# Neighbouring matmuls into different PSUM banks, in a fused attention, expert and gated-MLP kernel

## The chip, the cores and the metric

The kernel runs on one core of a Trainium2 chip. The metric is the device time in microseconds (us) of that core for one execution of the whole program. Times in the trace are counted from the start of its span; durations of single instructions are in nanoseconds (ns). The engines are PE (TensorE matmul), PEld (TensorE weight load), DVE (VectorE), ACT (ScalarE), POOL (GpSimd) and SP (the queue that issues most transfers).

## What is computed

Three layers follow one another, all in float32.

```python
# attention by features: q, k, v are 4 x 8 x 576 x 64, w_phi is 64 x 128
q_p, k_p = phi(q), phi(k)                    # exp(+-proj) with the row's maximum taken off
num = q_p @ (k_p.T @ v); den = q_p @ sum(k_p)
x = num / (den + 1e-6)                       # as 2304 tokens x 512

# 8 experts, two to a token, 512 -> 1024 -> 512
for e in range(8):
    h = maximum(x[mask] @ w1[e], 0.0)
    out[mask] += top2_w[mask] * (h @ w2[e])

# gated MLP over all tokens, 512 -> 1536 -> 512
xn = x / sqrt(mean(x * x) + 1e-6) * rms_g
g = xn @ w_gate
y = (g * sigmoid(g) * (xn @ w_val)) @ w_out
```

## The kernel before

Every large product is made of three matmuls for each pair of blocks: both operands are split into a high and a low part (`split`, line 120: ACT makes the high part, DVE the low part by subtraction), and high x high, high x low and low x high are added up in PSUM. Since 128 x 128 blocks are the stationary operand, each matmul has its own weight load.

PSUM is used in whole banks. `bank` (line 110) hands out 512-column tiles under two tags, np with five buffers and acc with three, each in rotation: a new tile takes the buffer of the tile of that tag that lies five (or three) calls back, and waits until that tile's last reader is done.

The work is issued in an order written out by hand. A long list (lines 24 to 46) orders attention and routing; from line 1168 on, loops do. Each engine takes its instructions strictly in that order, and so does SP's queue of transfers.

The first expert layer has 8 experts with two units of tokens each, of three and two tiles of 128 tokens. `s1_chunk` (line 786) makes one of 8 chunks of hidden values in one np bank. `s2_chunk` (line 804) adds chunk f to the unit's output, which has one acc bank for each tile of tokens; it finishes the three matmuls of a tile before it turns to the next tile. `y_out` (line 816) copies the banks out, DVE and ACT by turns, and POOL scatters the rows to `y_d`.

The gated MLP works on nine groups of 256 tokens. For each group, twelve calls of `g_chunk` (line 961) make 128 gate features and 128 value features each: one np bank holds both halves, the twelve matmuls of the gate half (L970) come first, those of the value half after them. Then ACT takes the sigmoid of the gate half (L974), and DVE multiplies it by the gate half (L975) and by the value half (L976). `g_split` (line 979) splits the product of the chunk before. Then `o_chunk` (line 984) adds chunk by chunk to the output of 128 tokens, in an acc bank for each of the group's two tiles (j): three matmuls (L991) for j = 0, three for j = 1, and so on. In the last group the steps are sorted, so that all of j = 0 is done before j = 1. `store` (line 994) copies an output and sends it out.

The MLP's weights are loaded during the last experts and the first group: `w_load` (line 664) issues the transfer on SP's queue, `w_hi` (line 682) makes the high part on ACT (for gate and value in four pieces scaled by the norm's weights, L691), `w_lo` (line 696) the low part on DVE (L702). In the loop over the first group's chunks they stand in the order `g_chunk(f)`, `g_split(f - 1)`, `w_lo`, `w_hi`, `w_load` (lines 1233 to 1242). The rows of the second group are fetched by `gather2(1)` (line 1230), ahead of the first group's chunks, from the rows that the experts have scattered.

Of the kernel before, what the change touches and what calls it, by code (L numbers as in the profile page):

```python
# [15 lines left out]
AF = mybir.ActivationFunctionType  # L16
# [5 lines left out]

# the order of attention and routing: each name stands for its function's next call
ORDER = """
# [25 lines left out]
def moe_stack_kernel(  # L50
# [17 lines left out]
    nc = tc.nc  # L68
# [41 lines left out]
    def bank(tag, *shape):  # L110
        n = 1
        for d in shape:
            n *= d
        t = ps.tile([P, 512], F32, name=tag, bufs=BUFS[tag])[:, 0:n]
        return t.rearrange("p (a b) -> p a b", a=shape[0]) if len(shape) > 1 else t
# [7 lines left out]

    # features 128 i + 32 kk + r lie at partitions 32 i + r where vector transposes make the operand
    def w1_src(e, kk):
# [6 lines left out]

    # ---------------------------------------------------------------- attention and routing
    aq_s, ak_s = ExitStack(), ExitStack()
# [47 lines left out]

    # the tensor engine's clock rises with use: products of no account until the first loads land
    warm = aq.tile([P, 512], BF16, name="warm")
# [53 lines left out]

    # An item is eight (head, token tile) blocks. k: heads of a quad, two tiles, or all heads of
    # a tail tile; q likewise. T transposes, H and L their two parts, P projection, M maximum,  # L240
    # U their maximum over features, X features, Z and Y sums of features, C contraction,
    # G, B and V copies, Q a tail's share, F the state by features; for queries V copies,
    # A maximum and S its subtraction, C contraction, N division.
    tps, xts, pps, pms, kp, kpt, acc, kvz = {}, {}, {}, {}, {}, {}, {}, {}
# [123 lines left out]

    # a head's columns: state by dimension, by the router's weights, feature sums
    def kF(it, c):  # L370
# [15 lines left out]

    # features of two heads a tile: pair i's heads A and B, or all pairs' head i for a tail
    def qP(it, i):
# [36 lines left out]

    # numerators, logits and denominators by tokens: a tile of the item, or half the heads of a tail
    def qC(it, i):
# [161 lines left out]

    # a pair's token row; an empty slot reads row 0  # L590
    def row_ids(ids, r):
# [6 lines left out]

    # ---------------------------------------------------------------- slots beyond CAP
    def overflow():  # L600
# [36 lines left out]

    # ---------------------------------------------------------------- experts
    nu = 2 * KF2 // 2 + KF2 // 2
# [22 lines left out]

    # an expert's unit lands in a tile of its own, the gated MLP's in the second half of its slot
    def w_load():
# [68 lines left out]
    ixs, rxs = (ix0, ix1), (rx0, rx1)  # L733
    # quarter rows by partitions 32 i + t: quarter i of the tokens of slots t
    rq = sp_.tile([P, E - 1, CAP // 32], I32, name="rq")
    quart = sp_.tile([P, 1], I32, name="quart")
    x_q = x_d.rearrange("t (i f) -> (t i) f", i=4)
    # an expert's units: 3 and 2 tiles, for expert 0 the smaller first
    groups = [(e, u) for e in range(E) for u in range(2)]
# [27 lines left out]

    # blocks of 32 transposed: features by partitions
    def turn(t, i, x, y):
# [16 lines left out]
    def s1_chunk(n, f):  # L786
        e, u = groups[n]
        N = P * NTL[n]
        t = xT[n][0]
        hp = bank("np", N)  # L790
        # the tokens' low parts are there last
        for m, (c, kk, a) in enumerate([(0, kk, a) for kk in range(KD) for a in range(2)]
                                       + [(1, kk, 0) for kk in range(KD)]):
            nc.tensor.matmul(hp, lhsT=slot1(e, kk)[:, a, f * P:(f + 1) * P], rhs=t[:, kk, c, :],  # L794
                             start=(m == 0), stop=(m == 3 * KD - 1))
        h = mp.tile([P, 2, NU0], F32R, name="hT", bufs=KF)[:, :, 0:N]
        nc.scalar.activation(out=h[:, 0, :], in_=hp, func=AF.Relu)  # L797
        nc.vector.scalar_tensor_tensor(out=h[:, 1, :], in0=hp, scalar=0.0, in1=f32(h[:, 0, :]),  # L798
                                       op0=ALU.max, op1=ALU.subtract)
        hT[n, f] = h  # L800
# [3 lines left out]
    def s2_chunk(n, f):  # L804
        e, u = groups[n]
        if f == 0:
            yacc[n] = [bank("acc", 512) for _ in range(NTL[n])]
        w = slot1(e, 4 + f // 2)
        h = hT.pop((n, f))
        o = (f % 2) * DM  # L810
        for i in range(NTL[n]):
            for m, (a, c) in enumerate(((0, 0), (0, 1), (1, 0))):
                nc.tensor.matmul(yacc[n][i], lhsT=h[:, a, i * P:(i + 1) * P], rhs=w[:, c, o:o + DM],  # L813
                                 start=(f == 0 and m == 0), stop=(f == KF - 1 and m == 2))
# [14 lines left out]

    # float64 weights arrive as pairs of words: exponent and fraction move to float32's places,  # L830
    # and what lies below float32's normal range becomes zero
    c64 = {}
# [49 lines left out]

    # ---------------------------------------------------------------- gated MLP
    NG2 = TT // 2
# [48 lines left out]

    # by way of DRAM: partitions 32 q + t take quarter q of the tokens t of each 32
    def put2(i):
# [25 lines left out]
    def g_chunk(i, f):  # L961
        t = xT["m2", i]
        gp = bank("np", 2, GN)
        for s_ in range(2):
            w = slot2[2 * (f // 2) + s_].rearrange("p c (k n) -> p c k n", k=KD)
            o = (f % 2) * P
            m = 0
            for kk in range(KD):
                for a, c in ((0, 0), (0, 1), (1, 0)):
                    nc.tensor.matmul(gp[:, s_, :], lhsT=w[:, a, kk, o:o + P], rhs=t[:, kk, c, :],  # L970
                                     start=(m == 0), stop=(m == 3 * KD - 1))
                    m += 1
        sg = mp.tile([P, GN], F32, name="sg", bufs=3)
        nc.scalar.activation(out=sg, in_=gp[:, 0, :], func=AF.Sigmoid)  # L974
        nc.vector.tensor_tensor(out=sg, in0=sg, in1=gp[:, 0, :], op=ALU.mult)  # L975
        nc.vector.tensor_tensor(out=sg, in0=sg, in1=gp[:, 1, :], op=ALU.mult)  # L976
        sgs[i, f] = sg
# [5 lines left out]

    def o_chunk(i, f, j):
        if f == 0:
            oacc[i, j] = bank("acc", 512)
        w = slot2[2 * (KF2 // 2) + f // 2]
        h = hT["m2", i, f]
        o = (f % 2) * DM
        for m, (a, c) in enumerate(((0, 0), (0, 1), (1, 0))):  # L990
            nc.tensor.matmul(oacc[i, j], lhsT=h[:, a, j * P:(j + 1) * P], rhs=w[:, c, o:o + DM],  # L991
                             start=(f == 0 and m == 0), stop=(f == KF2 - 1 and m == 2))

# [10 lines left out]

    # ---------------------------------------------------------------- order of work
    left, right = ExitStack(), ExitStack()
# [6 lines left out]

    # expert 0's first unit takes what the first batches gave it, up to its size; its second starts there
    def snap_mm():
# [119 lines left out]

    # loads follow the last use of what they replace
    follow = {}
# [91 lines left out]
    with tc.manual_schedule():  # L1229
        gather2(1)  # L1230
        for i in range(NG2):
            cpos = 1 if i else 5
            for f in range(KF2):
                g_chunk(i, f)
                if f:
                    g_split(i, f - 1)
                if halves:
                    w_lo()
                if raws:
                    w_hi()  # L1240
                if can_load():
                    w_load()
                if 0 <= f - cpos < 5 and i + 1 < NG2:
                    combine(i + 1, f - cpos)
                if i + 1 < NG2 and f == 9:
                    put2(i + 1)
                if i + 1 < NG2 and f == 11:
                    take2(i + 1)
            g_split(i, KF2 - 1)
            if i + 2 < NG2:  # L1250
                gather2(i + 2)
            # the last group's first tile is on its way out while the second is computed
            last = i == NG2 - 1
            steps = [(f, j) for f in range(KF2) for j in range(2)]
            if last:
                steps.sort(key=lambda t: t[1])
            for f, j in steps:
                o_chunk(i, f, j)
                if (f, j) == (3, 1) and not last:
                    trans2(i + 1)  # L1260
                if f == KF2 - 1:
                    store(i, j, 1 + last)
# [29 lines left out]
```

## Time and profile before

| | us |
|---|---|
| time, median of 3 runs | 1142.2 (1141.68 to 1142.35) |
| span of the profiled execution | 1135.5 |
| PE busy | 1098.5 (97%) |
| PE weight loads busy | 990.9 (87%) |
| DVE busy | 668.9 (59%) |
| ACT busy | 488.4 (43%) |
| POOL busy | 333.1 (29%) |

A share is an average over the stages. PE is busy for nearly all of the span, so it is the first engine to follow. The view to read is the chain of work that ended last, which shows at which places PE itself was held up; for every such place the view in order of time shows by whom. Matmuls are pipelined: the mean of one instruction is longer than the spacing from one to the next, so the spacing is read from a whole piece of work divided by its count.

### The profile page before, as it was taken

The page shows a single profiled execution, that of the slowest core. Times are in us where ns is not written, and L with a number is a line of the kernel's source. Part 1 is how long each engine was busy: PE and PEld are TensorE (multiplying, and loading weights), DVE is VectorE, ACT ScalarE, POOL GpSimd, SP SyncE. Part 2 cuts the span into 40 slices and gives each one's busy share as a digit, 9 for nine tenths or more (in the row PEclk, how much of TensorE's full clock was granted, in tenths as well). Part 3 has the DMA queues.
Part 4 walks back from the last instruction along what each step waited for, and adds up shares of the span by engine and source line. Part 5 has one row for each costly group of instructions (what it writes and reads, how often), then busy time and mean ns, then how long its engine had stood idle before and what let it go on. Part 6 is the DMA issues. An engine that isn't in the chain of part 4 may idle for free.

```text
span 1135.5 us, 20715 instructions
## 1 busy us (share of the span) xinstructions
PE 1098.5 (97%) x7985; PEld 990.9 (87%) x7985; DVE 668.9 (59%) x1438; ACT 488.4 (43%) x1142; POOL 333.1 (29%) x371
## 2 busy tenths in 40 slices
PE   8998899879899999999999999999999999999998
PEld 5777677769789898999999999899998989999997
DVE  6899999946557676767666657442333424343331
ACT  7989885423324343433434466232231323223121
POOL 2445666627545454545454020000000000000000
PEclk9999998899899999999999999999999999999999
DMA  9643303676366665665665345211211111121000
GB/s 177 137 104 79 82 20 122 151 184 197 118 180 197 197 205 182 204 197 184 204 204 186 145 148 194 93 48 48 74 43 58 60 47 47 48 67 33 31 20 19
DMA packets 125017, 134.39 MB, mean 118 GB/s; under 512 B 74690, under 2 KB 82882, under 8 KB 124912
## 3 DMA queue, kind: packets, MB, share of 16 engines
q1 hardware_dynamic: 115616, 112.97, 34.4%
q0 software_dynamic: 9296, 20.02, 5.5%
q8 instruction: 65, 1.06, 0.4%
q14 instruction: 40, 0.33, 0.1%
HBM read 100.41 MB, written 33.59 MB: 118 GB/s over the span
## 4 chain that ended last, share of the span: by engine, by line
PE 73%; DMA 0%; issue 0%; DVE 0%; ACT 0%; POOLq 0%
PE np L970 27%; PE acc L813 17%; PE np L794 16%; PE acc L991 13%; DMA xg<-x_d,rq 0%; PE np L957 0%; DVE hT L798 0%; ACT hT L797 0%; DVE y L1000 0%; ACT y L1000 0%; POOLq L608 0%
## 5 line engine op out<-in xcount | busy, mean ns | idle before, releaser
L752 POOL DMA_INDIRECT xg<-x_d,rq x140 | 153.9, 1099 | 52.7 <-issue 50.8
L970 PEld LDWEIGHTS np<-xT,wq 128*128 128x128 f32 x1296 | 154.6, 188 | 0.7
L970 PE MATMUL np<-xT,wr 128*128 128x256 f32 x1296 | 154.8, 281 | 0.0
L970 PE MATMUL np<-xT,wq 128*128 128x256 f32 x1296 | 154.8, 281 | 0.0
L970 PEld LDWEIGHTS np<-xT,wr 128*128 128x128 f32 x1296 | 154.0, 188 | 0.0
L975 DVE TENSOR_TENSOR sg<-sg,np 128x256 f32<-128x256 f32 x108 | 45.5, 421 | 170.7 <-ACT sg L974 170.6
L813 PE MATMUL acc<-wq,hT 128*128 128x512 f32 x540 | 126.7, 393 | 4.6 <-DVE hT L798 4.6
L794 PE MATMUL np<-xT,wq 128*128 128x384 f32 (+1 forms) x768 | 125.7, 312 | 5.2 <-DMA xg<-x_d,rq 5.2
L794 PE MATMUL np<-xT,wr 128*128 128x256 f32 (+1 forms) x768 | 124.2, 309 | 0.7 <-ACT xT L121 0.7
L813 PEld LDWEIGHTS acc<-wq,hT 128*128 128x128 f32 x540 | 101.6, 190 | 26.1 <-DVE hT L798 5.5
L794 PEld LDWEIGHTS np<-xT,wq 128*128 128x128 f32 x768 | 117.3, 191 | 6.1 <-issue 5.5
L974 ACT ACTIVATE sg<-np 128x256 f32<-128x256 f32 x108 | 41.5, 384 | 188.3 <-PE np L970 188.3
L925 POOL TENSOR_TENSOR ss<-ss,mhalf 128x1 f32<-128x1 f32 x18 | 9.7, 551 | 369.8 <-DVE ss L924 369.8
L794 PEld LDWEIGHTS np<-xT,wr 128*128 128x128 f32 x768 | 115.5, 188 | 1.6 <-ACT xT L121 0.8
L797 ACT ACTIVATE hT<-np 128x256 fp32r<-128x256 f32 (+1 forms) x128 | 55.7, 438 | 135.3 <-PE np L794 133.1
L798 DVE SCALAR_TENSOR_TENSOR hT<-np,hT 128x256 fp32r<-128x256 f32 (+1 forms) x128 | 62.3, 489 | 66.8 <-ACT hT L797 57.4
L411 POOL PARTITION_ALL_REDUCE am<-pc x36 | 75.5, 2115 | 84.1 <-ACT pc L405 71.9
L991 PE MATMUL acc<-wx,hT 128*128 128x512 f32 x432 | 99.5, 389 | 0.0
L813 PE MATMUL acc<-wr,hT 128*128 128x512 f32 x420 | 97.4, 390 | 0.0
L991 PEld LDWEIGHTS acc<-wx,hT 128*128 128x128 f32 x432 | 81.1, 188 | 16.8
L813 PEld LDWEIGHTS acc<-wr,hT 128*128 128x128 f32 x420 | 78.4, 188 | 15.8
L595 POOL DMA_INDIRECT y_d<-y,ix x40 | 41.0, 1025 | 165.4 <-DVE y L822 157.5
(185 smaller groups left out, 1651.2 us busy)
## 6 DMA issues: line engine op xcount, KB each, us to landing
raw<-in_moe_w_dram SPq DMA_DIRECT2D x36, 512.0 KB
raw<-in_moe_w_dram SPq DMA_DIRECT2D x112, 128.0 KB
m_d<-o SPq DMA_DIRECT2D x36, 256.0 KB
xg<-y_d SPq DMA_DIRECT2D x32, 256.0 KB
r<-in_moe_w_gate_dram SPq DMA_DIRECT2D x12, 512.0 KB
r<-in_moe_w_val_dram SPq DMA_DIRECT2D x12, 512.0 KB
r<-in_moe_w_out_dram SPq DMA_DIRECT2D x12, 512.0 KB
kq<-in_k_dram SPq DMA_DIRECT2D x32, 128.0 KB
```

Source lines behind the costliest of these rows:

```text
L411: nc.gpsimd.partition_all_reduce(am, pc, P, bass_isa.ReduceOp.absmax)
L595: return nc.gpsimd.indirect_dma_start(out=y_d[:, :], out_offset=bass.IndirectOffsetOnAxis(ap=ids, axis=0), in_=src, in_offset=None, bounds ...
L752: nc.gpsimd.indirect_dma_start(out=xg[n][t // 2][:, t % 2, g * P:(g + 1) * P], out_offset=None, in_=x_q, in_offset=bass.IndirectOffsetOnAx ...
L794: nc.tensor.matmul(hp, lhsT=slot1(e, kk)[:, a, f * P:(f + 1) * P], rhs=t[:, kk, c, :], start=(m == 0), stop=(m == 3 * KD - 1))
L797: nc.scalar.activation(out=h[:, 0, :], in_=hp, func=AF.Relu)
L798: nc.vector.scalar_tensor_tensor(out=h[:, 1, :], in0=hp, scalar=0.0, in1=f32(h[:, 0, :]), op0=ALU.max, op1=ALU.subtract)
L813: nc.tensor.matmul(yacc[n][i], lhsT=h[:, a, i * P:(i + 1) * P], rhs=w[:, c, o:o + DM], start=(f == 0 and m == 0), stop=(f == KF - 1 and m ...
L925: nc.gpsimd.tensor_tensor(out=ss, in0=ss, in1=mhalf, op=ALU.pow)
L970: nc.tensor.matmul(gp[:, s_, :], lhsT=w[:, a, kk, o:o + P], rhs=t[:, kk, c, :], start=(m == 0), stop=(m == 3 * KD - 1))
L974: nc.scalar.activation(out=sg, in_=gp[:, 0, :], func=AF.Sigmoid)
L975: nc.vector.tensor_tensor(out=sg, in0=sg, in1=gp[:, 0, :], op=ALU.mult)
L991: nc.tensor.matmul(oacc[i, j], lhsT=h[:, a, j * P:(j + 1) * P], rhs=w[:, c, o:o + DM], start=(f == 0 and m == 0), stop=(f == KF2 - 1 and m ...
```

## The change

`s2_chunk` turns its two loops round: for each of the three products it goes through the unit's tiles, so that neighbouring matmuls write to different banks. `g_chunk` takes two np banks, one for gate and one for value, and alternates between them matmul by matmul. `o_chunk` gets a list of tiles and alternates between their banks; the last group passes one tile at a time, as before. Sums, operands and the counts of matmuls stay as they are.

```diff
@@ s2_chunk
-        for i in range(NTL[n]):
-            for m, (a, c) in enumerate(((0, 0), (0, 1), (1, 0))):
+        for m, (a, c) in enumerate(((0, 0), (0, 1), (1, 0))):
+            for i in range(NTL[n]):
                 nc.tensor.matmul(yacc[n][i], lhsT=h[:, a, i * P:(i + 1) * P], rhs=w[:, c, o:o + DM],
                                  start=(f == 0 and m == 0), stop=(f == KF - 1 and m == 2))
@@ g_chunk
-        gp = bank("np", 2, GN)
-        for s_ in range(2):
-            w = slot2[2 * (f // 2) + s_].rearrange("p c (k n) -> p c k n", k=KD)
-            o = (f % 2) * P
-            m = 0
-            for kk in range(KD):
-                for a, c in ((0, 0), (0, 1), (1, 0)):
-                    nc.tensor.matmul(gp[:, s_, :], lhsT=w[:, a, kk, o:o + P], rhs=t[:, kk, c, :],
-                                     start=(m == 0), stop=(m == 3 * KD - 1))
-                    m += 1
+        gv = bank("np", GN), bank("np", GN)
+        ws = [slot2[2 * (f // 2) + s_].rearrange("p c (k n) -> p c k n", k=KD) for s_ in range(2)]
+        o = (f % 2) * P
+        for m in range(3 * KD):
+            kk, (a, c) = m // 3, ((0, 0), (0, 1), (1, 0))[m % 3]
+            for g_, w in zip(gv, ws):
+                nc.tensor.matmul(g_, lhsT=w[:, a, kk, o:o + P], rhs=t[:, kk, c, :],
+                                 start=(m == 0), stop=(m == 3 * KD - 1))
         sg = mp.tile([P, GN], F32, name="sg", bufs=3)
-        nc.scalar.activation(out=sg, in_=gp[:, 0, :], func=AF.Sigmoid)
-        nc.vector.tensor_tensor(out=sg, in0=sg, in1=gp[:, 0, :], op=ALU.mult)
-        nc.vector.tensor_tensor(out=sg, in0=sg, in1=gp[:, 1, :], op=ALU.mult)
+        nc.scalar.activation(out=sg, in_=gv[0], func=AF.Sigmoid)
+        nc.vector.tensor_tensor(out=sg, in0=sg, in1=gv[0], op=ALU.mult)
+        nc.vector.tensor_tensor(out=sg, in0=sg, in1=gv[1], op=ALU.mult)
@@ o_chunk
-    def o_chunk(i, f, j):
+    def o_chunk(i, f, js):
         if f == 0:
-            oacc[i, j] = bank("acc", 512)
+            for j in js:
+                oacc[i, j] = bank("acc", 512)
...
         for m, (a, c) in enumerate(((0, 0), (0, 1), (1, 0))):
-            nc.tensor.matmul(oacc[i, j], lhsT=h[:, a, j * P:(j + 1) * P], rhs=w[:, c, o:o + DM],
-                             start=(f == 0 and m == 0), stop=(f == KF2 - 1 and m == 2))
+            for j in js:
+                nc.tensor.matmul(oacc[i, j], lhsT=h[:, a, j * P:(j + 1) * P], rhs=w[:, c, o:o + DM],
+                                 start=(f == 0 and m == 0), stop=(f == KF2 - 1 and m == 2))
@@ the loop over groups
-            steps = [(f, j) for f in range(KF2) for j in range(2)]
-            if last:
-                steps.sort(key=lambda t: t[1])
-            for f, j in steps:
-                o_chunk(i, f, j)
-                if (f, j) == (3, 1) and not last:
-                    trans2(i + 1)
-                if f == KF2 - 1:
+            for js in ((0,), (1,)) if last else ((0, 1),):
+                for f in range(KF2):
+                    o_chunk(i, f, js)
+                    if f == 3 and not last:
+                        trans2(i + 1)
+                for j in js:
                     store(i, j, 1 + last)
```

## Rows read from the trace of the kernel before

**Rows 1.** The page's busy line and granted clock in 40 slices of the span
```profile
PE 1098.5 (97%) x7985; PEld 990.9 (87%) x7985; DVE 668.9 (59%) x1438; ACT 488.4 (43%) x1142; POOL 333.1 (29%) x371
...
PEclk9999998899899999999999999999999999999999
```

**Rows 2.** Chain that ended last, in time order: start us, us, what
```profile
653.61 11.36 PE np L794 x96
...
673.18 0.87 PE np L957 x8
...
676.83 34.08 PE np L970 x288
710.90 16.37 PE acc L991 x72
...
1114.48 16.38 PE acc L991 x72
```

**Rows 3.** Order of time, PE, first group: start us, us, instruction, [idle before]
```profile
676.66 17.20 PE L970 MATMUL np<-xT,wq 128*128 128x256 f32 x144
```

**Rows 4.** Order of time, ACT and DVE, one chunk of a later group
```profile
901.37 0.39 ACT L974 ACTIVATE sg<-np 128x256 f32<-128x256 f32 x1 [2.16 <-PE np L970]
...
901.79 0.42 DVE L975 TENSOR_TENSOR sg<-sg,np 128x256 f32<-128x256 f32 x1 [1.63 <-ACT sg L974]
```

**Rows 5.** Order of time, ACT, first group
```profile
691.85 1.71 ACT L691 ACTIVATE wr<-wr,g_sb 128x256 fp32r<-128x256 f32 x4 [5.79 <-DMA wr<-m_d]
693.47 0.36 ACT L974 ACTIVATE sg<-np 128x256 f32<-128x256 f32 x1
```

**Rows 6.** Order of time, DVE, first group
```profile
693.86 0.42 DVE L975 TENSOR_TENSOR sg<-sg,np 128x256 f32<-128x256 f32 x1 [5.27 <-ACT sg L974]
...
696.57 0.42 DVE L975 TENSOR_TENSOR sg<-sg,np 128x256 f32<-128x256 f32 x1
...
697.70 1.67 DVE L702 SCALAR_TENSOR_TENSOR wr<-wr,g_sb 128x256 fp32r<-128x256 f32 x4
699.28 0.41 DVE L975 TENSOR_TENSOR sg<-sg,np 128x256 f32<-128x256 f32 x1
...
705.12 0.42 DVE L975 TENSOR_TENSOR sg<-sg,np 128x256 f32<-128x256 f32 x1
```

**Rows 7.** Order of time, POOL and SP's queue, around the first group's start
```profile
680.06 0.98 POOL L595 DMA_INDIRECT y_d<-y,ix  x1 [0.22 <-issue]
...
682.92 1.74 SPq L907 DMA_DIRECT2D xg<-y_d  x4
684.77 1.06 SPq L679 DMA_DIRECT2D wr<-m_d  x2
```

**Rows 8.** PE order of time at waits; stretches: us, PE busy (x), PEclk, DMA share, GB/s
```profile
137.53 0.66 PE L261 MATMUL np<-ident,qq 128*128 128x128 f32 x4 [1.17 <-ACT kp L303]
...
141.97 0.96 PE L398 MATMUL np<-xt,wbd 128*128 128x256 f32 x6 [1.80 <-DVE pb L551]
...
299.34 6.43 PE L794 MATMUL np<-xT,wq 128*128 128x384 f32 x24 [5.16 <-DMA xg<-x_d,rq]
...
130.00:139.80 9.80, 8.63 (x110) 1.00 0.39 110
143.40:146.60 3.20, 3.20 (x14) 0.50 0.12 49
...
297.00:303.60 6.60, 4.26 (x13) 0.50 0.42 134
```

**Rows 9.** Order of time, two PE waits and a DVE row, first expert
```profile
238.95 0.42 DVE L798 SCALAR_TENSOR_TENSOR hT<-np,hT 128x256 fp32r<-128x256 f32 x1
...
239.42 3.90 PE L813 MATMUL acc<-wq,hT 128*128 128x512 f32 x10 [4.65 <-DVE hT L798]
...
244.12 0.66 PE L783 MATMUL np<-ident,xg 128*128 128x128 f32 x4 [0.80 <-DMA xg<-x_d,rx]
```

## The prediction

> **What bounds the kernel now.** I read the page's busy line and clock line first: TensorE (PE) is busy 97% of the span, and from the middle on each slice shows it full at a granted clock of 0.9 or more [rows 1]. So I turned next to the chain that ended last, in order of time [rows 2]. From about 300 us to the end it is a single string of PE pieces without a wait between them, ending in two short copies. The reader is to see two things there. First, any time that PE waits after that point is added to the end in full, and anything that ACT, DVE or a queue does costs nothing as long as PE doesn't wait for it. Second, the pieces give the spacing of matmuls: 34.08 us / 288 = 118.3 ns for the 256-column matmuls of the gated part (L970), and 16.37 / 72 = 227.4 ns for the 512-column ones of the output product (L991).
>
> **Step 1: what alternation itself is worth.** The edit adds and removes no matmul: 24 a chunk in g_chunk, 6 a step in o_chunk, 6 or 9 a step in s2_chunk, as before. It could pay only if a matmul that follows one into the same bank starts later than one that follows a matmul into another bank. The trace of before holds both kinds. In groups 0 to 7 the output product changes bank every 3 matmuls (23 changes in 72); in the last group it does 36 into one bank and then 36 into the other (1 change). The two pieces take 16.37 and 16.38 us [rows 2]. So 22 more changes are worth at most some 0.01 us, 0.5 ns each, with either sign. The edit adds about 3500 changes: 108 x 23 less the few that were there in the gated part, 8 x 12 x 4 in the output product, and some 600 in s2_chunk. I take 0 for them, and keep 3500 x 0.5 ns = 1.7 us on both sides as the bound. In the gated part the bank changed only between chunks; 288 matmuls of a group make a smooth 34.08 us, so nothing is hidden at the joints either.
>
> [...]
>
> **Step 2: what the gated part now asks of the banks.** The tag np has 5 banks in rotation. Before, a chunk took one; now it takes two, one for gate and one for value. Counting the rotation on: the value bank of chunk f is the gate bank of chunk f-2, and the gate bank of chunk f is the value bank of chunk f-3. A bank is free when its last reader is done: for gate the first multiply (L975, after the sigmoid L974), for value the second (L976). So the second matmul of chunk f waits for L975 of chunk f-2. Between the end of chunk f-2 and that matmul there is one chunk, 24 x 118.3 = 2.84 us. Before, there were four.
>
> In groups 1 to 8 this is enough: the sigmoid starts as PE ends its chunk, and L975 ends 901.79 + 0.42 - 901.37 = 0.84 us later [rows 4]. The slack is about 1.9 us; cost 0.
>
> In group 0 it is not enough. ACT also splits the gated weights there, and stands 5.79 us in its queue, until 691.85, for the transfer of a weight tile (L691, <-DMA wr) [rows 5]. The sigmoid of chunk 3 is queued behind that split and starts at 693.47, though PE had passed from chunk 3 to chunk 4 at 676.66 + 96 x 0.1183 = 688.02; L975 of chunk 3 ends at 693.86 + 0.42 = 694.28 [rows 6]. PE needs that bank for the second matmul of chunk 5: 676.66 + 121 x 0.1183 = 690.98 us [rows 3, 2]. In the kernel before this delay was hidden, because the bank came back round only five chunks later. Now PE stands. A release by DVE reached PE 0.05 us after the end of the DVE instruction (238.95 + 0.42 to 239.42) [rows 9], so the matmul starts at 694.33: a wait of 3.35 us. To this I add 0.1 us for the weight load, which no longer runs ahead; its bounds are 0 and the spacing of the shortest matmuls, 0.87 / 8 = 0.11 us [rows 2]. Sum: **3.45 us**.
>
> Could the landing move? The transfer was issued at 684.77 behind four gathers (682.92), and those follow the last scatter, issued at 680.06 [rows 7]. All of that lies ahead of the stall and hangs on the end of the experts, which the edit leaves where it was. I give it 0.5 us either way.
>
> Does it happen again? With the resumption at 694.43, chunk 6's value matmul comes at 694.43 + 24 x 0.1183 = 697.27, and its bank is free at 696.57 + 0.42 = 696.99. Chunk 7: 700.11 against 699.28 + 0.42 = 699.70. Chunk 9: 705.79 against 705.12 + 0.42 = 705.54 [rows 6]. So one wait gives PE enough delay for the rest; the margins are 0.25 to 0.4 us, so a second small wait is possible, but no more than some tenths.
>
> The value weights are needed 11 matmuls (1.3 us) earlier. The last such tile is split from 697.70 to 699.37 on DVE [rows 6] for chunk 10, which starts at 676.66 + 240 x 0.1183 = 705.05 even without the stall: cost 0, with 5.7 us of cover.
>
> **Step 3: the clock behind the wait.** [...] In the slow stretch after the 5.16 us wait PE worked 4.26 us at half clock, which lost 2.1 us; in the one after 1.80 us it worked 3.20 us, which lost 1.6 [rows 8]. Part of such a stretch may fall into the wait and cost nothing. I take **1.4 us**, near the smaller; bounds 0 (the clock holds) and 3.2 (twice the smaller row).
>
> **Step 4: the other two products.** In s2_chunk the low half of the hidden values is now needed at the fifth or seventh matmul in place of the third. In steady running PE never waits for it. It did once, for 4.65 us before 239.42 [rows 9], and PE can now do two more matmuls ahead of that wait. But the next PE work after it waits for gathered rows (244.12 <-DMA xg) [rows 9], so those 0.5 to 0.9 us go into that wait: 0. Each y bank now ends 1 to 4 matmuls later, under 1 us, and its copies have an s1 stage of 11.36 us (L794) [rows 2] before the bank is asked for again. The last expert's scatter hangs on a DVE copy that follows other DVE work, not on the order of the banks. o_chunk delays the first store of groups 0 to 7 by two matmuls, with a gated part of 34 us behind it. The last group is computed as before, so the tail is the same. All 0.
>
> **The sum.** Span 1135.5 + 3.45 + 1.4 = 1140.35 us; what lies around the span is 1142.2 - 1135.5 = 6.7 us against the median, so **1147.0 us**, 0.4% slower.
>
> **The rivals.**
> A (forecast): one wait in group 0 and a slow clock behind it, 1146.1 to 1149.3. For it: the rows of ACT and DVE are unaffected by PE in that stretch, and PE has no wait later that could take the delay back.
>
> B: the wait, but the clock holds: 1142.2 + 3.45 = 1145.7, between 1145.1 and 1146.1. For it: the granted clock also stayed up after some waits of about 1 us [rows 8].
> [...]
>
> C: no wait forms. Its place is the weight tile's landing: the stall is what the landing (691.85) lies behind 688.5, so a landing 3.4 us earlier removes it, as would a schedule in which chunk 3's sigmoid stands ahead of that split. Time 1142.2, within 1.7 us. Against it: the order of ACT's instructions in the text is unchanged, and 7.1 us from issue to use has little reason to halve.
>
> D (the other side, faster): matmuls into the same bank do hinder each other, and the joints hide it. The floor is the spacing of the eight transposes, 108.8 ns [rows 2]: (118.3 - 108.8) x 2592 = 24.6 us, so 1117.6. It decides as soon as the saved spacing is over 1.9 ns (4.85 us / 2592). Against it stand the equal 16.37 and 16.38 us.
>
> **How the numbers follow.** Chances: A 0.54, B 0.26, C 0.14, D 0.06. A difference of about 0.2%, 2.3 us, is what a measurement of this kernel can tell from none, so A and B are slower (0.80), C the same (0.14), D faster (0.06). A and B alone hold 0.80 from 1145.1 to 1149.3, and their own bounds leave some of that out; so the range goes down to C's value: 1142.2 to 1149.3.
>
> **What would show it.** Right: in the new trace one PE row in the first gated group with idle time of about 3.3 us, put down to DVE L975 (or its new line), about 14 us after that group's start; the other eight groups at 34.08 us and the output products at 16.37; a slice of lower clock just behind the wait. Wrong: the wait is absent or several times as large; waits recur in groups 1 to 8; or the spacing of 118.3 ns has changed, which would overturn step 1.

## The result and the profile after

The changed kernel takes 1147.92 us (median of 9 runs, 1145.89 to 1151.54), the kernel before 1142.2 us in the runs made beside them (9 runs, 1137.1 to 1144.98). The ratio is 1.0057, 95% interval 1.0041 to 1.0072: 4.7 to 8.2 us slower. Ratios here are not quotients of the two medians; they are formed from the runs of each kernel that lie within 1.5% of its fastest, which is every run on this chip, but only 17 of the 35 of the kernel before on the second chip, so that ratios from there lean upward.

The first view is the chain that ended last in the changed kernel, around the first gated group and in one later group (start us, us, what):

```profile
680.46 2.73 PE np L969 x23
683.21 0.39 ACT sg L972
...
688.40 7.17 DMA wr<-m_d
...
697.20 0.37 ACT sg L972
697.57 0.02 issue
697.59 0.43 DVE sg L973
698.02 0.04 issue
698.07 21.54 PE np L969 x167
719.60 16.33 PE acc L992 x72
735.94 34.08 PE np L969 x288
770.02 16.37 PE acc L992 x72
...
1123.14 16.38 PE acc L992 x72
```

Before, this stretch was one string of PE pieces [rows 2]. Now the chain leaves PE in the first group, goes back through DVE's multiply and ACT's sigmoid to the transfer of a weight tile, and returns to PE at 698.07. From then on each piece is as long as before: 34.08, 16.37 and, in the last group, 16.38 us.

The second view is the order of time, PE, ACT and DVE in that group, then SP's queue:

```profile
680.30 14.47 PE L969 MATMUL np<-xT,wq 128*128 128x256 f32 x121
698.07 4.29 PE L969 MATMUL np<-xT,wq 128*128 128x256 f32 x23 [3.30 <-DVE sg L973]
...
719.44 5.62 PE L992 MATMUL acc<-wq,hT 128*128 128x512 f32 x24
...
695.59 1.70 ACT L691 ACTIVATE wr<-wr,g_sb 128x256 fp32r<-128x256 f32 x4 [6.01 <-DMA wr<-m_d]
697.20 0.36 ACT L972 ACTIVATE sg<-np 128x256 f32<-128x256 f32 x1
...
697.59 0.42 DVE L973 TENSOR_TENSOR sg<-sg,np 128x256 f32<-128x256 f32 x1 [5.41 <-ACT sg L972]
...
686.55 1.75 SPq L907 DMA_DIRECT2D xg<-y_d  x4
688.40 0.85 SPq L679 DMA_DIRECT2D wr<-m_d  x2
```

PE does exactly 121 matmuls, five chunks of 24 and the first of chunk 5, then stands 3.30 us until DVE has read the gate bank of chunk 3. The rows of ACT, DVE and SP are those of before [rows 5 to 7], 3.6 to 3.7 us later on the clock of the span: counted from the group's first matmul, the tile lands after 15.29 us now and 15.19 us before. The first group's gated part takes 719.44 - 680.30 = 39.14 us in place of 34.08, 5.06 us more.

The third view is PE's busy time and granted clock in two stretches behind the wait (stretch, us, PE busy, PEclk, DMA share, GB/s):

```profile
699.40:702.60 3.20, 3.20 (x17) 0.50 0.92 369
702.80:719.40 16.60, 16.60 (x142) 1.00 0.09 35
```

From 1.2 us behind the resumption on, the granted clock was 0.50 for some 3.4 us (699.3 to 702.7). There 12 matmuls took 2.56 us (their starts from 699.59 to 702.15), 213 ns each in place of 118.3; over 3.4 us that is a loss of 1.5 us (an estimate from these starts). The resumption itself came 3.46 us late: 698.07 against 680.30 + 121 x 0.1183 = 694.61. The other 1.60 us of the 5.06 lie behind the resumption and are put, nearly all, to the slow clock; an experiment below tests this.

The spans of the two profiled executions differ by 8.7 us (1135.5 and 1144.2), and 3.64 us of this lie ahead of the gated part (first matmul at 676.66 and 680.30). These are no effect of the edit: in the second experiment all that runs ahead of the gated part is as in the kernel before, and its gated part begins at 682.30. The stages ahead of the gated part vary from execution to execution, and the profiled execution of before was an early one.

### The profile page after: what moved, and what is told of

Same layout as the page of the kernel before. It is cut to its first block, busy times and chain, and to the rows that moved or that the text cites. A ratio compares the mean times of both kernels' runs of the same rounds, so it can differ in the third digit from the quotient of the medians.

```text
span 1144.2 us, 20830 instructions
## 1 busy us (share of the span) xinstructions
PE 1101.4 (96%) x7985; PEld 992.8 (87%) x7985; DVE 667.3 (58%) x1438; ACT 488.4 (43%) x1142; POOL 328.9 (29%) x371
## 4 chain that ended last, share of the span: by engine, by line
PE 72%; DMA 1%; ACT 0%; SPq 0%; issue 0%; DVE 0%
PE np L969 26%; PE acc L813 17%; PE np L794 16%; PE acc L992 13%; DMA wr<-m_d 1%; DMA raw<-in_moe_w_dram 0%; DMA y_d<-y,ix 0%; SPq L907 0%; ACT wr L691 0%; PE np L957 0%; ACT sg L972 0%; DVE y L1001 0%; DVE sg L973 0%; ACT y L1001 0%; SPq L608 0%
## 5 line engine op out<-in xcount | busy, mean ns | idle before, releaser
L752 POOL DMA_INDIRECT xg<-x_d,rq x140 | 148.4, 1060 | 54.2 <-issue 51.7
L969 PEld LDWEIGHTS np<-xT,wr 128*128 128x128 f32 x1296 | 154.4, 189 | 0.0
L794 PE MATMUL np<-xT,wr 128*128 128x256 f32 (+1 forms) x768 | 126.7, 313 | 0.7 <-ACT xT L121 0.7
L794 PEld LDWEIGHTS np<-xT,wr 128*128 128x128 f32 x768 | 118.0, 191 | 1.8 <-ACT xT L121 0.9
```

The costliest lines, as they stand in the source:

```text
L752: nc.gpsimd.indirect_dma_start(out=xg[n][t // 2][:, t % 2, g * P:(g + 1) * P], out_offset=None, in_=x_q, in_offset=bass.IndirectOffsetOnAx ...
L969: nc.tensor.matmul(g_, lhsT=w[:, a, kk, o:o + P], rhs=t[:, kk, c, :], start=(m == 0), stop=(m == 3 * KD - 1))
```

## The experiments

All of them are compared with runs of the kernel before made beside them. The more exact measure is the length of group 0 in the profile, from its first gated matmul to its first output matmul, since the varying stages ahead of it don't enter: 34.08 us before, 39.14 after.

**One bank in group 0 alone.**

```diff
+        if i == 0:
+            gp = bank("np", 2, GN)
...
+            gv = gp[:, 0, :], gp[:, 1, :]
+        else:
             gv = bank("np", GN), bank("np", GN)
```

> The changed kernel, but in group 0 of the gated MLP a chunk keeps one bank for both halves and does gate first, then value; the other eight groups and both output products keep the alternation. Theory T (the whole loss is PE waiting in group 0 for the bank of chunk 3, and the slow clock behind it): group 0 takes 34.1 us from its first gated matmul to its first output matmul, as in the kernel before (39.1 in the changed one), no PE wait by the sigmoid's chain, time as before within 2 us (some 1142). Rival R1 (each change of bank costs a little, everywhere): the eight other groups still alternate, so some 8/9 of the loss stays, 1146 to 1148.

Measured: 1142.69 us against 1141.82, ratio 0.9999 (0.9989 to 1.0009). The chain, first two groups:

```profile
682.83 34.08 PE np L971 x288
716.91 16.37 PE acc L1005 x72
733.28 34.08 PE np L982 x288
```

L971 is the old form, one bank and no turns; L982 the alternating one. They take the same time to the last digit, and with group 0 put back the whole loss is gone, though the tile landed late here too, 14.66 us after the group's start (697.33 - 682.67). R1 falls: eight groups that alternate cost nothing.

**The gated part alone.** The kernel before with the new `g_chunk`; `s2_chunk`, `o_chunk` and the loop stay as they were.

> The kernel before with the gated part's alternation alone; both output products stay as they were. T: the same loss as the whole change: group 0 takes 38 to 39.2 us, one PE wait of about 3.3 us, time 4 to 6 us over before. Rival R2 (a share of the loss sits in the first experts' second product, whose new order shifts waits and the clock around 240 us): the time is 1 to 3 us below that of the changed kernel, though group 0 is as long.

Measured: 1147.11 us, ratio 1.0036 (1.0019 to 1.0053), that is 2.2 to 6.1 us over before. PE in order of time, ACT's split of the late weight tile, and three stretches of PE's clock:

```profile
682.30 14.47 PE L969 MATMUL np<-xT,wq 128*128 128x256 f32 x121
699.94 4.34 PE L969 MATMUL np<-xT,wq 128*128 128x256 f32 x23 [3.17 <-DVE sg L973]
...
697.46 1.70 ACT L691 ACTIVATE wr<-wr,g_sb 128x256 fp32r<-128x256 f32 x4 [5.89 <-DMA wr<-m_d]
...
240.40:247.10 6.70, 4.25 (x10) 0.50 0.66 130
250.60:257.20 6.60, 5.85 (x20) 0.50 0.90 284
701.20:704.40 3.20, 3.20 (x17) 0.50 0.96 383
```

The same wait after the same 121 matmuls, and a group 0 of 39.02 us. The slow clock around 250 us, which the changed kernel's profile also had (0.50 for 13.50 us, 242.00 to 255.50), is here for 13.2 us in two stretches without the new order in `s2_chunk`, so it needs no new order. The interval of the time doesn't by itself exclude R2; the next run does better.

**The other products alone.** The changed kernel with the old `g_chunk`.

> The changed kernel with the gated part as it was before: only the two output products alternate. T: no difference from before within 2 us, group 0 at 34.1 us, and the output products of groups 0 to 7 at 16.37 us. R2: 1 to 3 us slower than before, and in the profile a longer slow clock between 240 and 260 us, as the changed kernel's profile had it.

Measured: 1142.28 us, ratio 0.9999 (0.9988 to 1.0010); group 0 takes 34.08 us, the output product 16.37. The slow clock around 242 us is in this profile too (13.7 us long; 3.4 us in that of before), and the time is still that of before. As the same old order shows 3.4 us in the one profile and 13.2 in the other (the run above), its length varies with the execution, and R2 falls. In the two output products alternation neither gains nor costs what could be measured.

**Weights ahead of the rows.**

```diff
-        gather2(1)
...
+                if (i, f) == (0, 3):
+                    gather2(1)
```

> The changed kernel, in which the fetch of the second group's rows is issued after chunk 3 of group 0, so that the first four of the weight transfers stand ahead of it in SP's queue and need not wait for the experts' last scatter. All alternation stays. T (the cause is ACT standing for the weight tile): the tile lands 4 us or more earlier, the sigmoid of chunk 3 starts as PE ends that chunk, the wait falls to under 0.5 us, group 0 takes 34.1 to 34.6 us, time as before within 2 us. Rival R3 (two banks a chunk are too few by themselves, whatever the transfers do): the wait stays over 2 us.

Measured: 1141.77 us, ratio 0.9994 (0.9983 to 1.0005). ACT, then PE in order of time:

```profile
690.53 0.38 ACT L972 ACTIVATE sg<-np 128x256 f32<-128x256 f32 x1 [0.56 <-PE np L969]
690.81 0.40 ACT L121 CAST hT<-sg 128x256 fp32r<-128x256 f32 x1
691.10 1.71 ACT L691 ACTIVATE wr<-wr,g_sb 128x256 fp32r<-128x256 f32 x4
693.37 0.39 ACT L972 ACTIVATE sg<-np 128x256 f32<-128x256 f32 x1 [0.56 <-PE np L969]
...
681.93 17.20 PE L969 MATMUL np<-xT,wq 128*128 128x256 f32 x144
698.97 17.20 PE L969 MATMUL np<-xT,wr 128*128 128x256 f32 x144
```

The split of the weights no longer waits, the sigmoid of chunk 3 (693.37) follows PE at once, PE doesn't stop, and group 0 is back at 34.08 us with every alternation in place. R3 falls: two of five banks a chunk are enough where ACT isn't held up. This version isn't faster than the kernel before either.

**Turns within one bank.**

```diff
-        gv = bank("np", GN), bank("np", GN)
+        gp = bank("np", 2, GN)
+        gv = gp[:, 0, :], gp[:, 1, :]
...
-                                 start=(m == 0), stop=(m == 3 * KD - 1))
+                                 start=(m == 0 and s_ == 0), stop=(m == 3 * KD - 1), skip_group_check=True)
```

> The changed kernel, but gate and value alternate matmul by matmul within the two halves of one bank, so that a chunk again takes one bank of the five. The order of the matmuls is that of the change, only their place differs. T: the order costs nothing and the bank count is what costs, so group 0 takes 34.1 us without a wait and the time is as before within 2 us. Rival R1 (turning between gate and value weights and sums is itself slower): the gated parts of groups 1 to 8 take over 34.2 us each.

This and the three runs below were made on another chip, on which the kernel before takes 1201.87 us (1183.92 to 1221.61); the extra time lies ahead of the gated part, which began at 733 to 737 us, and the groups are as long as on the first chip. The changed kernel itself wasn't run on it. Times here tell little, stages tell as much as before. Measured: 1203.02 us, 1.15 us over before by the medians; the ratio, 1.0067 (1.0016 to 1.0118), is over before by more than was expected. All the gated part is as short as it was:

```profile
737.00 34.08 PE np L970 x288
771.08 16.37 PE acc L993 x72
```

The tile landed 15.12 us after the group's start (751.96 - 736.84), as late as before, and PE didn't stand. So in the part that was edited neither T's one bank nor R1's turns cost anything. The ratio above 1 has no place in this trace's edited stages. With before itself spread over 38 us and the ratio leaning upward, the runs don't show that this version is slower; whether it is stays open.

**The wait filled.**

```diff
+        if (i, f) == (0, 5):
+            idle = bank("acc", GN)
+            for _ in range(28):
+                nc.tensor.matmul(idle, lhsT=slot2[0][:, 0, 0:P], rhs=t[:, 0, 0, :], start=True, stop=True)
```

> The changed kernel, with 28 matmuls of no account (256 columns, into a free bank of the other tag) ahead of chunk 5 of group 0: 28 x 118.3 ns = 3.3 us, as long as the wait, so that PE works where it stood. T (the loss is the wait plus a slow clock that the wait brings): the wait is still lost, but the granted clock stays up; group 0 takes 37.4 to 37.6 us (34.08 + 3.3 + at most 0.2) in place of 39.1, and the time is some 1.7 us below the changed kernel's, 3 to 4 us over before. Rival R4 (the rest of the loss behind the wait is not the clock but late banks): group 0 stays at 39 us.

Measured: 1199.48 us, 2.4 us under before by the medians, though the ratio is 1.0054 (1.0016 to 1.0093); such a spread can't test the forecast of the time. The chain, PE's clock behind the filled stretch, then ACT and DVE:

```profile
733.72 14.20 PE np L973 x120
747.92 3.32 PE acc L966 x28
751.23 19.88 PE np L973 x168
771.11 16.34 PE acc L996 x72
...
747.70:760.00 12.30, 12.30 (x106) 1.00 0.66 267
...
748.29 1.71 ACT L691 ACTIVATE wr<-wr,g_sb 128x256 fp32r<-128x256 f32 x4 [5.46 <-DMA wr<-m_d]
...
750.30 0.42 DVE L977 TENSOR_TENSOR sg<-sg,np 128x256 f32<-128x256 f32 x1 [4.86 <-ACT sg L976]
```

PE never stands, the granted clock stays at 1.00, and group 0 takes 37.39 us: 34.08 and the 3.31 us of the 28 matmuls, nothing else. Against 39.14 us that is 1.75 us: the 1.60 us behind the wait are gone, and the matmuls are 0.15 us shorter than the 3.46 us by which the resumption was late. R4 falls. In this execution the tile came earlier, 748.29 - 733.56 = 14.73 us after the group's start where it was 15.29, and DVE had freed the bank at 750.72, before the 28 matmuls ended. So they were longer than the wait that they stood in for, which would have been shorter by about the same 0.56 us as the tile came earlier (an estimate); the price of standing, beyond the wait itself, is the 1.60 us and not the whole 1.75.

**One fetch twice, in the changed kernel and in that of before.**

```diff
                 for sl, rows in rows_of(t, y_d, j * NP2):
-                    nc.sync.dma_start(out=pr[j][sl, h, :], in_=rows)
+                    for _ in range(2 if (i, h, j) == (1, 0, 0) else 1):
+                        nc.sync.dma_start(out=pr[j][sl, h, :], in_=rows)
```

> The changed kernel, in which one of the four fetches of the second group's rows is issued twice, ahead of the weight transfers, so that the weight tile lands later by D (some 1 to 4 us, to be read from its ACT row). T: the wait grows by D, one for one, from 3.3 us, and group 0 takes 39.1 + D or up to 1.7 us more or less as the clock falls; time 1 to 5 us over the changed kernel's. Rival R3 (the wait comes from the count of banks and not from the landing): group 0 stays at 39 us.

> The kernel before with the same doubled fetch, so that its weight tile lands later by the same D. T: with one bank a chunk the sigmoid may be late by two more chunks, 4.7 us, before PE asks for the bank, so group 0 stays at 34.1 us and the time as before within 2 us, as long as D is under 4.7. R3 makes no other forecast here; if group 0 grows by D too, the banks are not what hides a late weight tile in the kernel before, and T falls.

Measured: 1205.27 us, ratio 1.0094 (1.0042 to 1.0145), for the changed kernel, 1198.13 us, ratio 1.0000 (0.9946 to 1.0053), for that of before. First the changed kernel (ACT, PE, and a stretch of PE's clock), then, in the second fence, the kernel before (ACT, PE):

```profile
753.88 1.70 ACT L691 ACTIVATE wr<-wr,g_sb 128x256 fp32r<-128x256 f32 x4 [8.29 <-DMA wr<-m_d]
...
736.32 14.47 PE L970 MATMUL np<-xT,wq 128*128 128x256 f32 x121
756.36 5.08 PE L970 MATMUL np<-xT,wq 128*128 128x256 f32 x23 [5.56 <-DVE sg L974]
...
778.31 5.63 PE L993 MATMUL acc<-wq,hT 128*128 128x512 f32 x24
...
754.30:761.00 6.70, 4.64 (x21) 0.50 1.02 411
```

```profile
752.83 1.71 ACT L691 ACTIVATE wr<-wr,g_sb 128x256 fp32r<-128x256 f32 x4 [8.83 <-DMA wr<-m_d]
...
734.60 17.20 PE L971 MATMUL np<-xT,wq 128*128 128x256 f32 x144
751.64 17.20 PE L971 MATMUL np<-xT,wr 128*128 128x256 f32 x144
768.68 5.65 PE L992 MATMUL acc<-wq,hT 128*128 128x512 f32 x24
```

In the changed kernel the tile lands 753.88 - 736.32 = 17.56 us after the group's start, 2.27 us later than in the changed kernel's profile on the first chip, and PE's wait grows from 3.30 to 5.56 us, by 2.26. Group 0 takes 41.99 us: 34.08, the 5.73 us by which the resumption was late (756.36 against 736.32 + 14.31 = 750.63), and 2.18 us behind it, where PE worked 4.64 us at a granted clock of 0.50. In the kernel before the tile lands 18.23 us after the start, 3.04 us later than in its own profile, and group 0 takes the same 34.08 us. A late tile costs one for one in the one kernel, and one later still costs nothing in the other: the banks that lie between a chunk and the next use of its bank are what hid it.

## Why the prediction was right, point by point

The forecast was case A, 1147.0 us; measured were 1147.92. The mechanism, its place, and its two terms are as forecast; that the wait fits to 0.01 us is in part luck.

**Step 1, alternation is worth 0.** Held. The spacing is 118.3 ns in three forms: halves one after the other in one bank (34.08 us a group), turns in one bank, turns between two banks; and 227.4 ns in the output product with a change after each matmul. The bound of 1.7 us to both sides was not needed. No run here shows a gain from a second bank for neighbouring matmuls. Rival D, which would have needed 1.9 ns a matmul, is out.

**Step 2, the wait.** Held: forecast 3.45 us (3.35 and 0.1 for the weight load), measured 3.46 us from the due start of the matmul to its start, at the forecast matmul (the second of chunk 5), released by the forecast multiply. What set it was shown from both sides: an earlier tile removes it, a later one lengthens it one for one. In the three profiles with a wait the resumption is late by the tile's landing less 11.83 us each time, counted from the group's start: 15.29 and 3.46 in the changed kernel, 15.16 and 3.33 with the gated part alone, 17.56 and 5.73 with the second fetch. The fit to 0.01 us is partly luck: the multiply ended 0.09 us later after the group's start than before (17.71 against 17.62), and PE's row began 0.06 us behind it (697.59 + 0.42 to 698.07), without the 0.1 us for the weight load. That load did not run ahead, as forecast: it began at 698.07 too. The second matmul began 0.22 us after the first (698.07 to 698.29), the third 0.12 us after the second, so some 0.1 us fell there, ahead of the slow clock; that the load took it is not shown. The landing moved by more than the 0.5 us allowed: with the transfers left as they were it came between 14.34 us (the other products alone) and 15.29. No second wait formed, as the ladder of chunks 6, 7 and 9 said; its thinnest margins of 0.25 to 0.4 us were not tried, since the slow clock behind the wait widened them.

**Step 3, the clock.** Held, a little small: 1.4 us were forecast, 1.60 measured, and 2.18 behind the longer wait. That a wait of this length would bring the clock down was the author's estimate from [rows 8]. The three profiles with the wait of 3.17, 3.30 and 5.56 us all show the granted clock at 0.50 behind it (in the longest it had fallen some 2 us before the wait ended), and the one where PE worked through the same time shows 1.00 (747.70 to 760.00). So rival B, that the clock holds, did not occur in any of them. The forecast reckoned half of the time worked at 0.50 as lost; the changed kernel's rows show 213 ns a matmul in place of 118.3, a loss of 95 in 213. In its gated part the trace shows one such fall, behind the one wait of 3.30 us, and none in groups 1 to 8, which go through the banks as fast: the granted clock was 1.00 from 735.70 to 1140.00, PE was busy for 403.81 of those 404.30 us, and the gated parts take 34.08 us each.

**Rival C** (the landing early enough) is what the weights-first run made true: there the tile was split 9.17 us after the group's start (691.10 - 681.93), ahead of the forecast turning point of 688.5 - 676.66 = 11.84 us, and the wait was gone. The three waits above put that point at 11.83.

**Step 4, the other products at 0.** Held: 0.9999 with them alone. PE now does ten matmuls ahead of the wait around 235 us in place of eight, but the work behind it still waits for gathered rows (0.68 us before 245.09), as the forecast said [rows 9].

**The sum.** One term was wrong, though it didn't move the forecast: "what lies around the span is 6.7 us". The runs list a span beside each time, and 1.7 us lie around it (1145.89 and 1144.2 for the profiled run of the changed kernel). With the span of 1135.5, the profiled execution of before must have been one of about 1137.2 us, as fast as the fastest of the nine (1137.1), and 5 us under the median. Adding to the median was right because the terms are differences; adding to the span would have told of an execution that was early for other reasons.

What stays open is the rest of the mean difference. The ratio says 4.7 to 8.2 us, the group's own rows 5.06 us in the one execution that was profiled. By the rule of 11.83 us, landings of 14.34 to 15.29 us would make the resumption 2.5 to 3.5 us late (an estimate from those rows), and the clock's part varies too. The interval holds 5.06, and nothing else in the profiles asks for more.

## What to carry to other kernels

When an edit makes each step of a loop take more buffers of a rotating pool, count how many steps now lie between a buffer's last use and its next claim, and compare that time with the latest release in the whole trace, not with the usual one: here the usual 0.84 us left 1.9 us to spare, and a single 6 us delay in one of nine groups caused the whole loss. Slack that looks idle can be cover for a transfer elsewhere, as it was for the weight tile that landed 15.19 us after the group's start before; with that cover used up, DVE, which PE had not waited for in that group, became the releaser of a wait of 3.30 us. Before giving buffers for a finer alternation, look in the trace of before for the same alternation where it already occurs; equal pieces with 1 and 23 changes of bank (16.38 and 16.37 us) said that there was nothing to gain.

## What the runs showed of the hardware

Here standing cost more than working: 28 matmuls of no account (3.31 us) in place of a resumption that was 3.46 us late made group 0 1.75 us shorter; the granted clock stayed at 1.00, and the 1.60 us that were lost behind the wait were not lost. The same program took 1142 us on one chip and 1202 on the other, while the gated groups took 34.08 and the output products 16.37 us on both (on the second chip in that kernel with the second fetch); the difference lies in the stages ahead of the gated part. From the long wait for gathered rows near 300 us to the gated part it is 377.3 us in the profile of the kernel before (299.34 to 676.66) and 420.9 on the second chip in that kernel with the second fetch (313.71 to 734.60). There PE stands for 17.1 us in waits for which the profile shows no releaser and 6.0 us for ACT, and on the first chip not at all; why wasn't tried.
